# Graph hops with gathering and scattering alternating on the tensor engine: one change and its blind prediction

## The chip, the cores and the metric

The kernel runs on one core of a Trainium2 chip. A core has five engines with a queue of instructions each: PE (the tensor engine: matmuls, with separate loads of their stationary matrix, "PEld" in the profile), DVE (the vector engine), ACT (the scalar engine), POOL (GpSimd) and SP (the sync engine, used here to issue DMAs). They wait for one another through semaphores. PE reads SBUF and writes PSUM; DVE and ACT read PSUM and write SBUF. The metric is the time of one execution in microseconds (us) on the device. An instruction's time in the profile is from its start to its end; on one engine the next may start before the last has ended.

## What is computed

The reference takes 10,000 nodes with 128 features and 160,000 directed edges. It makes seven "hops", each a sum over incoming edges, and then runs a small attention over the eight vectors (input and seven hops) of each node.

```python
h = x
toks = [x]
for _ in range(K):                                   # K = 7
    msg = h[src] * deg_inv_sqrt[src, None] * deg_inv_sqrt[dst, None]
    h = _segment_sum(msg, dst, N)
    toks.append(h)
tok = jnp.stack(toks, axis=1)                        # (N, 8, 128)
t = _layernorm(tok)
q, key, v = t @ wq, t @ wk, t @ wv
o = tok + (softmax(q @ key.T / sqrt(D)) @ v) @ wo    # per node, over its 8 tokens
alpha = softmax(_layernorm(o) @ w_r)
out = sum over the 8 tokens of alpha * o
```

The edges are the same in each hop. The change touches hops 2 to 7 only (and the copies of hop 1).

## The kernel before

**Tables and tiles.** The node values of a hop lie in SBUF as a table `tab` of 79 tiles of 128 nodes. Each value is kept as two float16 numbers, a high half and a low half, so an entry has 256 columns. Two tables take turns: a hop reads one and writes the other.

**A hop as matmuls.** For each of the 79 tiles of destination nodes, the edges into it were sorted once into 18 "slot tiles" of 128 edges; slot tile J takes 32 edges from each of four table tiles. What does not fit goes through two indirect DMAs (the "fetched" rows, `og`). One matrix `w` per destination tile, in 8-bit floats and with only zeros and ones, holds everything: 19 scatter matrices of 128x128 and 72 gather matrices of 128x32. It is stored in DRAM in hop 1 (`gsd`) and read back by SP in each later hop, into one of five buffers.

- *Gather* (L578): four matmuls with 128x32 matrices pick the 4 x 32 rows of one slot tile out of four table tiles and put them side by side into a PSUM tile `p`. Two slot tiles make a pair, with one `p` (128 x 512); nine pairs make a destination tile. There are six `p` buffers.
- *Copy* (L581): ACT or DVE copies `p` to an SBUF buffer `eb`, as float16. There are fourteen of these.
- *Scatter* (L554): one matmul with a 128x128 matrix adds a slot tile of `eb` into the PSUM tile `acc` (two buffers) of the destination tile. The two fetched tiles are added in the same way (L540; L567 for the first two tiles of a hop, whose second fetch comes late, as `ogl`).

**Closing a tile.** DVE adds the two halves of `acc` to `s` (L569). ACT makes the high half of the next table's entry (L610), DVE the low half (L611) and the largest magnitude per row (L612). The finished rows are stored to DRAM (`tabd`, L159, and for the first seven tiles also `tabh`, L163) for the indirect DMAs of the next hop; ACT issues that store. POOL scales `s` to the hop's result `r` (L619), and SP stores it (`tok`, L621).

**What sets the order.** In `block`, hops 2 to 7 call for all nine gathers of a tile in one run (`runs` is `(9,)`). Then `begin` opens `acc` with the fetched rows, and what is pending is scattered, except for the last two pairs, which with the closing step stay pending until after the next tile's gathers. At the end of a hop everything pending is worked off. ACT has pairs 0, 2, 4, 5 and 7 of a tile, DVE 1, 3, 6 and 8. A scheduler places the instructions on their queues; each queue then runs in its order. For a tile in the middle of a hop the queues hold:

- PE: 72 gather matmuls, 2 fetched, 18 scatter (the first four of them belong to the tile before).
- DVE: three copies, one copy, `s`, low half, maximum.
- ACT: five copies, high half, row store.
- POOL: a one-column copy that times the next fetch (L523), one indirect DMA, another one, `r`.
- SP: load of `w`, store of `tok`.

At a hop's start the scale of the next table is made from the maxima of the last one (`scale`), with small steps on DVE and PE, and the first tiles wait for the last rows of the hop before to land in `tabd`.

## Time and profile before

Three runs took 4150.82, 4152.88 and 4153.82 us, median 4152.88. The profiled execution is another one; its span, from the first to the last instruction of the program, is 4139.7 us, at a mean granted tensor clock of 0.976.

| engine | busy us | share of the span | instructions |
|---|---|---|---|
| PE matmul | 3818.7 | 92% | 69690 |
| PE load | 3021.9 | 73% | 69690 |
| DVE | 3355.8 | 81% | 6960 |
| ACT | 2692.1 | 65% | 6830 |
| POOL | 1769.2 | 43% | 2342 |

The preparation and hop 1 last until about 1200 us, hops 2 to 7 until about 3460 us, and the rest is mostly the attention. A row of the groups gives line, engine, operation, tiles (out<-in), shapes and count, then after a bar the busy time in us and the mean of one in ns, then after another bar the idle time of the engine just before and what ended it. A row of a timeline gives start and duration in us, engine, line, operation and count, and in brackets the idle time before it. "128*32" at a matmul is the shape of its stationary matrix. A shape such as 128x256 behind it is that of the result's free size. "Issue" as a releaser means that the engine waited for nothing the profile can name.

### The profile page before, as it was taken

What the parts mean: (1) busy time and instruction counts of PE and PEld (TensorE: products, weight loads), DVE (VectorE), ACT (ScalarE), POOL (GpSimd) and SP (SyncE); (2) the same over time, 40 slices, a digit from 0 to 9 for tenths busy, and PEclk for the clock granted to TensorE, in tenths of its full rate; (3) what the DMA queues carried; (4) which work ended last, traced back from release to release, by engine and by line L of the source; (5) the groups of instructions that cost most, each with busy time, mean ns of one, the idle gap of its engine ahead of it and who ended that gap; (6) DMA issues with size and microseconds to landing.
All of it is one profiled execution on the core that took longest, in us unless ns stands there. A gap on an engine that the chain in (4) does not pass through costs nothing. (4 is left out here: it accounts for less than half of the span.)

```text
span 4139.7 us, 164058 instructions
## 1 busy us (share of the span) xinstructions
PE 3818.7 (92%) x69690; PEld 3021.9 (73%) x69690; DVE 3355.8 (81%) x6960; ACT 2692.1 (65%) x6830; POOL 1769.2 (43%) x2342
## 2 busy tenths in 40 slices
PE   5886889999989999999999999999999999999997
PEld 4665666666657777777777777777777887788785
DVE  8998999999967777777677777777775665999998
ACT  6883456666656665666566566656665657888885
POOL 0000333343345555555555555555555663222222
PEclk8998999999999999999999999999999999999998
DMA  3000444554556665665566656656666653222220
GB/s 109 23 2 17 143 148 153 152 157 150 158 163 185 186 184 180 185 185 184 179 184 186 181 183 186 186 176 186 187 185 191 188 184 105 75 72 81 72 77 17
DMA packets 321181, 594.87 MB, mean 144 GB/s; under 512 B 56183, under 2 KB 214101, under 8 KB 315189
## 3 DMA queue, kind: packets, MB, share of 16 engines
q1 hardware_dynamic: 220565, 478.42, 37.0%
q0 software_dynamic: 35392, 72.55, 6.4%
q10 hardware_dynamic: 64480, 33.33, 2.8%
q8 instruction: 546, 8.95, 0.9%
q14 instruction: 198, 1.62, 0.1%
HBM read 455.43 MB, written 128.67 MB: 141 GB/s over the span
## 5 line engine op out<-in xcount | busy, mean ns | idle before, releaser
L581 ACT CAST eb<-p 128x512 f16<-128x512 f32 x3065 | 1591.8, 600 | 670.9 <-PE p L578 575.6
L581 DVE CAST eb<-p 128x512 f16<-128x512 f32 x1912 | 1263.9, 688 | 439.1 <-PE acc L554 271.6
L578 PE MATMUL p<-tab,w 128*32 128x256 f16 x39816 | 1371.3, 275 | 105.0 <-ACT eb L581 38.1
L578 PEld LDWEIGHTS <-w 128*32 128x32 fp8e4 x39816 | 999.0, 96 | 406.7 <-issue 349.4
L554 PE MATMUL acc<-eb,w 128*128 128x256 f16 (+1 forms) x9954 | 1247.3, 274 | 9.2 <-ACT eb L581 2.3
L554 PEld LDWEIGHTS <-w 128*128 128x128 fp8e4 x9954 | 953.8, 98 | 172.7 <-issue 57.4
L524 POOL DMA_INDIRECT og<-tabh,oidx x553 | 616.6, 1115 | 769.2 <-DVE vi L476 389.0
L524 POOL DMA_INDIRECT og<-tabd,oidx x541 | 584.0, 1080 | 599.9 <-PE acc L554 262.7
L610 ACT ACTIVATE tab<-s,c 128x128 f16<-128x128 f32 x395 | 158.7, 402 | 359.7 <-DVE eb L581 262.9
L619 POOL TENSOR_SCALAR r<-s,ctok 128x128 f32<-128x128 f32 x474 | 295.7, 624 | 45.3 <-DVE s L569 28.2
L611 DVE SCALAR_TENSOR_TENSOR tab<-s,c,tab 128x128 f16<-128x128 f32 x395 | 139.0, 352 | 182.8 <-issue 166.5
L523 POOL COPY og<-eb 128x1 f16<-128x1 f16 x452 | 84.0, 186 | 422.7 <-ACT eb L581 422.7
L569 DVE TENSOR_REDUCE s<-acc 128x128 f32<-128x256 f32 x553 | 228.9, 414 | 23.1 <-PE acc L567 10.1
L991 ACT ACTIVATE junk<-tab 128x128 f32<-128x128 f32 x625 | 245.2, 394 | 0.0
L338 ACT ACTIVATE rs<-iof,rb 128x128 fp8e4<-128x128 f32 x784 | 231.9, 393 | 0.3
L512 DVE TENSOR_TENSOR w<-dsl,iof 128x2432 fp8e4<-128x2432 f16 x79 | 211.6, 2678 | 0.0
L977 PEld LDWEIGHTS po<-v,pT 128*128 128x128 f32 x1250 | 159.3, 193 | 43.6 <-issue 27.8
L966 PE MATMUL pv<-Wv,xT 128*128 128x131 f32 x1250 | 175.9, 283 | 2.5 <-ACT xT L946 1.5
L1049 POOL TENSOR_TENSOR p<-e,in 128x512 f32<-128x512 f32 (+1 forms) x40 | 40.8, 1021 | 320.7 <-DVE e L1047 320.7
L977 PE MATMUL po<-v,pT 128*128 128x128 f32 x1250 | 166.9, 277 | 7.0 <-DVE tab L983 5.4
L966 PEld LDWEIGHTS pv<-Wv,xT 128*128 128x128 f32 x1250 | 152.9, 191 | 19.3 <-issue 8.3
L540 PE MATMUL acc<-og,w 128*128 128x256 f16 x553 | 156.6, 283 | 0.0
(284 smaller groups left out, 4598.7 us busy)
## 6 DMA issues: line engine op xcount, KB each, us to landing
w<-gsd SPq DMA_DIRECT2D x474, 592.0 KB
gsd<-w SPq DMA_DIRECT2D x79, 592.0 KB
rb<-srow SPq DMA_DIRECT2D x79, 576.0 KB
tok<-r SPq DMA_DIRECT2D x546, 64.0 KB
tab<-tok SPq DMA_DIRECT2D x273, 128.0 KB
tabd<-tab ACTq DMA_DIRECT2D x395, 64.0 KB
og<-tabh,oidx POOLq DMA_INDIRECT x553
og<-tabd,oidx POOLq DMA_INDIRECT x541
```

The source lines that it names most:

```text
L338: A.activation(ro[:, j - a, i, :], self.iof, AF.Abs_reciprocal_sqrt, scale=2.0 ** 21, bias=rb[:, j - VP, i:i + 1], saturate=False)
L512: V.tensor_tensor(w[:, :NJ * 128].rearrange("p (j d) -> p j d", d=128), dsl[:, g, :, None].to_broadcast([128, NJ, 128]), self.iof1[:, None ...
L524: self.nc.gpsimd.indirect_dma_start(out=o, out_offset=None, in_=src[0] if i == NI else src[1], in_offset=bass.IndirectOffsetOnAxis(ap=self ...
L554: T.matmul(acc[0][:, :m], w[:, J * 128:(J + 1) * 128], e[:, j, :m], start=first and J == 0, stop=J == NG - 1 and not (first or late))
L569: V.tensor_reduce(s, acc[0][:, 0:256].rearrange("p (h d) -> p d h", h=2), axis=X, op=ALU.add)
L578: T.matmul(p[32 * q:32 * q + 32, j], w[:, NJ * 128 + s * CAP:NJ * 128 + (s + 1) * CAP], tab[:, s, :], start=True, stop=True)
L581: (A.copy if evac(jj) else V.tensor_copy)(e[:, :n, 0:256], p[:, :n].rearrange("p j h d -> p j (h d)"))
L610: self.nc.scalar.activation(new[:, t, 0:128], s, AF.Copy, scale=c)
L619: self.nc.gpsimd.tensor_scalar(r, s, ct[:, t:t + 1], None, op0=ALU.mult)
L966: T.matmul(p[:, g - a, :], S[i]["xT"][:, g, :], Wv, start=True, stop=True)
L977: T.matmul(p[:, g - a, :], PT[i % 2][:, g, :], S[i]["v"][:, g, :128], start=True, stop=True)
L991: A.activation(j, S[i]["x"][:, g, :], AF.Square, bias=S[i]["x"][:, g, 0:1], scale=-1.0, accum_out=S[i]["sq"][:, g:g + 1])
```

## The change

Hop 1 keeps `block`. Hops 2 to 7 get a function of their own, `flow`. It does this:

- It alternates pair by pair: gather a pair, then scatter the pair four places earlier (`LAG`), across the borders of tiles and of hops. Nothing is worked off at a hop's end but the last.
- Each 128x128 scatter matrix, and each of the two fetched ones, is cut into four 128x32 matrices (`quarters`), each with a quarter of the result's partitions, at the same four places in the array that the gather uses. All matmuls of hops 2 to 7 (but a few small ones at a hop's start) thus have one shape.
- ACT copies the even pairs (0, 2, 4, 6, 8), DVE the odd ones. DVE's copy is written as a product with a column of ones, in `block` too.
- A tile's close is followed by `r` at once; the high half of the entry comes one pair later, the low half, the maximum and the store of the rows two pairs later (`steps`). SP issues that store instead of ACT.

```diff
-            (A.copy if evac(jj) else V.tensor_copy)(e[:, :n, 0:256], p[:, :n].rearrange("p j h d -> p j (h d)"))
+            pv = p[:, :n].rearrange("p j h d -> p j (h d)")
+            if evac(jj):
+                A.copy(e[:, :n, 0:256], pv)
+            else:
+                V.tensor_tensor(e[:, :n, 0:256], pv, self.one[:, :, None].to_broadcast([128, n, 256]), op=ALU.mult)
...
+    def flow(self, n, t, w, tab, og, pend, steps, evac, fin, late, mid, ahead, after):
...
+        def quarters(out, W, rows, start, stop):
+            for q in range(0, 128, 32):
+                T.matmul(out[q:q + 32], W[:, q:q + 32], rows, start=start, stop=stop, tile_position=(0, q))
+
+        def fetched(i, start=False, stop=False):
+            W = w[:, (NG + i) * 128:(NG + i + 1) * 128] if i < NI else self.Sov[:, t, :]
+            quarters(acc[0], W, og[i], start, stop)
+
+        def scat(e, jj):
+            if not acc:
+                acc.append(self.pacc.tile([128, 512], F32, name="acc", tag="acc")[:, :256])
+                for i in range(NI if late else NI + 1):
+                    fetched(i, start=i == 0)
+            for j in range(e.shape[1]):
+                J = 2 * jj + j
+                quarters(acc[0], w[:, J * 128:(J + 1) * 128], e[:, j, :256], False, J == NG - 1 and not late)
...
+        for jj in range(-(-NG // 2)):
...
+            for step in steps:
+                step[0] -= 1
+            while steps and not steps[0][0]:
+                steps.pop(0)[1]()
+            pend.append((1, lambda e=e[:, :m], jj=jj: scat(e, jj)))
+            while pend and (not pend[0][0] or sum(k for k, _ in pend) > LAG):
+                pend.pop(0)[1]()
...
-                def fin(t, s, acc, k=k, ct=ct, last=last, i=i):
+                def fin(t, s, k=k, ct=ct, last=last, i=i):
+                    self.token_out(k, t, s, ct)
                     if not last:
-                        self.entries(t, s, i)
-                        self.rows(1 - i, self.tab[1 - i], t, t + 1, nc.scalar)
-                    self.token_out(k, t, s, ct)
+                        steps.append([1, lambda: self.entries_hi(t, s, i)])
+                        steps.append([2, lambda: (self.entries_lo(t, s, i), self.rows(1 - i, self.tab[1 - i], t, t + 1, nc.sync))])
...
-                    for _ in self.block(t, w, tab, og[n], pend, 2, (9,), False, lambda jj: jj in (0, 2, 4, 5, 7), fin, n == 0, n < 2,
-                                        (lambda part, n=n: scale(part, n)) if n < 2 and not last else None,
-                                        lambda after=None, n=n: ahead(n, after), after):
-                        pass
-                while pend:
-                    pend.pop(0)()
+                    self.flow(n, t, w, tab, og[n], pend, steps, lambda jj: jj % 2 == 0, fin, n < 2,
+                              (lambda part, n=n: scale(part, n)) if n < 2 and not last else None,
+                              lambda after=None, n=n: ahead(n, after), after)
+            while pend:
+                pend.pop(0)[1]()
```

In the order built from this, DVE's queue holds per tile: copy 3, `s`, low half, copy 5, maximum, copy 7, and the next tile's copies 1 and 3. SP's holds the load of a `w`, the store of `tok`, the store of the rows.

More of the change, by code (lines that the diff above doesn't have):

```diff
@@ L36 @@
 KO = 8
+LAG = 4
 BIG = 32768.0
@@ L75, in __init__ @@
         V.memset(self.ones32, 1.0)
+        self.one = cp.tile([128, 1], F32, name="one")
+        V.memset(self.one, 1.0)
         self.ones16 = cp.tile([128, 1], F16, name="ones16")
@@ L605, in block, with close @@
             yield
-    def entries(self, t, s, i):
+    def flow(self, n, t, w, tab, og, pend, steps, evac, fin, late, mid, ahead, after):
+        V, A, T = self.nc.vector, self.nc.scalar, self.nc.tensor
+        acc = []
+        def quarters(out, W, rows, start, stop):
[12 more added lines that the diff above has]
+                quarters(acc[0], w[:, J * 128:(J + 1) * 128], e[:, j, :256], False, J == NG - 1 and not late)
+        def close():
+            if late:
+                fetched(NI, stop=True)
+            s = self.fp.tile([128, 128], F32, name="s")
+            V.tensor_reduce(s, acc[0].rearrange("p (h d) -> p d h", h=2), axis=X, op=ALU.add)
+            fin(t, s)
+        for jj in range(-(-NG // 2)):
+            m = min(2, NG - 2 * jj)
+            p = self.pg.tile([128, 2, 2, 128], F32, name="p")
+            for j in range(m):
+                for q in range(4):
+                    s = 4 * (2 * jj + j) + q
+                    T.matmul(p[32 * q:32 * q + 32, j], w[:, NJ * 128 + s * CAP:NJ * 128 + (s + 1) * CAP], tab[:, s, :], start=True, stop=True)
+            e = self.ebuf[self.eb_i % len(self.ebuf)]
+            self.eb_i += 1
+            pv = p[:, :m].rearrange("p j h d -> p j (h d)")
+            if evac(jj):
+                A.copy(e[:, :m, 0:256], pv)
+            else:
+                V.tensor_tensor(e[:, :m, 0:256], pv, self.one[:, :, None].to_broadcast([128, m, 256]), op=ALU.mult)
+            if jj == 0 and not late:
+                ahead(e[:, 0, 0:1])
+            for step in steps:
[5 more added lines that the diff above has]
+                pend.pop(0)[1]()
+            if jj == 4 and n == 1 and mid:
+                mid(0)
+        if n == 0 and mid:
+            mid(0)
+            mid(1)
+        if late:
+            ahead()
+        if after:
+            after[1]()
+        pend.append((0, close))
@@ L609, in entries, with entries_hi, entries_lo @@
+    def entries_hi(self, t, s, i):
+        self.nc.scalar.activation(self.tab[1 - i][:, t, 0:128], s, AF.Copy, scale=self.c1[i][:, t:t + 1])
+    def entries_lo(self, t, s, i):
         c, new = self.c1[i][:, t:t + 1], self.tab[1 - i]
-        self.nc.scalar.activation(new[:, t, 0:128], s, AF.Copy, scale=c)
         self.nc.vector.scalar_tensor_tensor(new[:, t, 128:256], s, c, new[:, t, 0:128], op0=ALU.mult, op1=ALU.subtract)
@@ L699, in run @@
             self.more_ebufs(c.enter_context(tc.tile_pool(name="eb2", bufs=1)), 9, False)
-            pend = []
+            pend, steps = [], []
             for k in range(2, nhop + 1):
```

## The prediction

> **What bounds the kernel now.** I read the stretches first, cut at the first finished sum (`s`) of each hop, then the timeline of one tile, then hop 7's tile against it, then the groups. The first and the last hop's stretch and the sum of all six (busy us and count of PE, PEld, DVE, ACT, POOL; clock, DMA share, GB/s):

> ```profile
> 1206.70:1587.40 380.70, 366.60 (x7314) 294.59 (x7306) 281.08 (x573) 232.87 (x474) 218.49 (x312) 1.00 0.60 184
> ...
> 3112.30:3458.80 346.50, 341.98 (x7089) 287.28 (x7081) 223.99 (x387) 202.87 (x385) 212.41 (x307) 0.99 0.59 182
> sum 2252.10, PE 2168.31 PEld 1753.48 DVE 1620.89 ACT 1367.05 POOL 1302.51; mean PE 361.38 PEld 292.25 DVE 270.15 ACT 227.84 POOL 217.09
> ```

> Hops 2 to 7 take 2252.1 us, 79 tiles each. PE is nearly always busy, at full clock; the others are not. But PE's busy time holds the latencies of matmuls that overlap, so one tile's timeline has to say what PE lacks:

> ```profile
> 2501.31 0.41 DVE L569 TENSOR_REDUCE s<-acc 128x128 f32<-128x256 f32 x1
> 2501.76 0.40 ACT L610 ACTIVATE tab<-s,c 128x128 f16<-128x128 f32 x1 [0.99 <-DVE eb L581]
> 2501.96 1.31 PEld L578 LDWEIGHTS <-w 128*32 128x32 fp8e4 x49 [0.21 <-issue]
> 2501.96 2.53 PE L578 MATMUL p<-tab,w 128*32 128x256 f16 x72
> ...
> 2502.19 0.35 DVE L611 SCALAR_TENSOR_TENSOR tab<-s,c,tab 128x128 f16<-128x128 f32 x1 [0.47 <-issue]
> 2502.46 0.28 DVE L612 TENSOR_REDUCE mx<-tab 128x1 f32<-128x128 f16 x1
> 2502.57 0.35 ACTq L159 DMA_DIRECT2D tabd<-tab  x1
> 2502.63 0.32 SPq L621 DMA_DIRECT2D tok<-r  x1
> 2502.70 2.04 DVE L581 CAST eb<-p 128x512 f16<-128x512 f32 x3
> 2502.96 2.54 ACT L581 CAST eb<-p 128x512 f16<-128x512 f32 x5 [0.81 <-PE p L578]
> 2503.60 0.60 PEld L578 LDWEIGHTS <-w 128*32 128x32 fp8e4 x23 [0.33 <-issue]
> ...
> 2504.42 0.10 PEld L540 LDWEIGHTS <-w 128*128 128x128 fp8e4 x1 [0.21 <-issue]
> ...
> 2504.65 2.13 PE L554 MATMUL acc<-eb,w 128*128 128x256 f16 x18
> 2505.43 0.69 DVE L581 CAST eb<-p 128x512 f16<-128x512 f32 x1 [0.69 <-PE acc L554]
> ...
> 2506.04 0.41 DVE L569 TENSOR_REDUCE s<-acc 128x128 f32<-128x256 f32 x1
> ```

> A tile lasts 2506.04 - 2501.31 = 4.73 us. The loads idle 0.21 us at each change between 128x32 and 128x128 matrices, and the gather's loads break off after 49, until 2503.60. The cause of the break is on ACT: it runs the entry (2501.76), its row store then has to wait for DVE's low half (2502.19) and is issued at 2502.57, and only behind it comes the first copy, at 2502.96, 1.0 us after the gather began. By then six `p` buffers are full and the seventh pair waits. Hop 7, which makes no entries, shows the tile without that:

> ```profile
> 3300.08 2.15 PE L578 MATMUL p<-tab,w 128*32 128x256 f16 x72
> ...
> 3302.39 2.13 PE L554 MATMUL acc<-eb,w 128*128 128x256 f16 x18
> 3304.45 2.15 PE L578 MATMUL p<-tab,w 128*32 128x256 f16 x72
> ```

> Here a tile takes 4.37 us. Eighteen full matrices cost (2.13 - 0.27)/17 = 0.109 us each, where 0.27 is one matmul's latency; eighteen groups of four quarter matrices (2.15 - 0.28)/17 = 0.110, less a trifle for the staggered starts, so 0.109 again. A tile is 18 gathered, 18 scattered and 2 fetched: PE's pure work is 38 x 0.1093 = 4.15 us. The rest of hop 7's tile, 0.22, is the two changes of shape; 4.73 - 4.37 = 0.36 is the wait behind the row store.

> **The change, part by part.**

> *Quarters in place of full matrices.* The 20 matrices of 128x128 become four 128x32 each: PE's matmuls with their loads go from 2 x 92 = 184 to 2 x 160 = 320 a tile. New is that all four of a group stream the same rows, which no gather does. The attention does, in L1003:

> ```profile
> L997 PE MATMUL ps<-xT,uT 128*32 128x32 f32 x5000 | 51.3, 198 | 0.3
> ...
> L1017 DVE TENSOR_TENSOR c<-ps,in 128x512 f32<-128x512 f32 x39 | 26.5, 679 | 0.0
> L1003 PE MATMUL sm<-rb,same 128*32 128x256 f32 x312 | 25.1, 391 | 2.6 <-DVE rb L1010 2.6
> ```

> Its 312 are 78 groups of four, two to a visit: (25.1 - 39 x 0.39)/39 = 0.25 us for the second group, in f32. Were the four to take turns, one would have to pass in 0.06 us, and no 256 columns in these rows do. Bounds of a scatter group: 0.109, below which no 256 columns in these rows go, and 0.25. I take 0.109, the gather's, which has our types and lengths. [...]

> *One shape within a tile.* Two changes go, 0.22 us in each of 474 tiles. If turning from gathering to scattering cost something by itself, less would go; I take the whole.

> *Alternation, four pairs apart.* PE's order becomes gather j, scatter j-4. From a gather's last issue to its scatter there are now 8 x 0.219 = 1.75 us. The copy between needs 0.16 (rest of the matmul's 0.27) + 0.69 and two hand-overs of 0.05 (ACT's first copy ends at 2502.96 + 0.60, the loads go on at 2503.60): 0.95. So DVE or ACT may be 0.8 us late before PE feels it.

> *The entry split, its row store on SP.* ACT loses the 0.35 us issue and the wait ahead of it, so the 0.36 goes unless something else is late. SP gets the store between a token store and a load of `w`, 0.32 + 0.35 + 0.32 us of issues in 4.15. Behind its wait for the low half stands that load:

> ```profile
> w<-gsd SPq DMA_DIRECT2D x474, 592.0 KB
> ```

> It has five buffers and so some 3.6 tiles, 15 us, to land; 592 KB at the 184 GB/s of the stretch are 3.3 us, which is what a tile would pay at worst if that cover were gone. DMA must move the same bytes in 4.15 for 4.73: 210 GB/s, share 0.68, not full. In the first seven tiles a second store goes the same way.

> What is late next is DVE. Its order per tile is: copy 3, `s`, low half, copy 5, maximum, copy 7, copies 1 and 3. Start to start by the rows: copy 0.61 (2505.43 to 2506.04), `s` to low half 0.88 (with ACT's entry between), low half 0.27, maximum 0.24. Sum 4 x 0.61 + 0.88 + 0.27 + 0.24 = 3.83, under 4.15. The tightest place is copy 7. Counted from the last issue of gather 3 it is ready at 0.21 + 0.61 + 0.88 + 0.27 + 0.61 + 0.24 + 0.69 + 0.05 = 3.56 us; its scatter is due at 4 x 0.437 + 0.22 + 1.75 = 3.72. It fits, with 0.16 to spare. ACT and POOL do too: ACT has five copies of 0.604 and the entry's 0.40, 3.42; POOL's stretch gives 218.49/79 = 2.77.

> *Copies as products.* L1017 is such a product (f32 from PSUM by a broadcast), 679 ns, against 688 for the copy:

> ```profile
> L581 DVE CAST eb<-p 128x512 f16<-128x512 f32 x832 | 553.2, 688 | 163.6 <-PE acc L554 130.2 <-PE p L578 18.4 <-remote 4.6
> L581 ACT CAST eb<-p 128x512 f16<-128x512 f32 x1039 | 530.1, 604 | 195.1 <-PE p L578 181.2 <-DVE eb L581 9.0 <-remote 3.3
> ```

> Nine ns on an engine with time left: nothing. In hop 1 only the last quad's copies are DVE's.

> *Hop edges.* A hop costs 380.7 - 79 x 4.73 = 7 us over its tiles, hop 7 346.5 - 79 x 4.37 = 1.3. The emptying of the pipeline at each end goes. The first tiles of a hop must still wait until the last rows have landed and been gathered:

> ```profile
> 1963.59 2.13 PE L554 MATMUL acc<-eb,w 128*128 128x256 f16 x18
> 1968.44 0.27 PE L567 MATMUL acc<-ogl,Sov 128*128 128x256 f16 x1 [2.73 <-DMA ogl<-tabd,oidx]
> ```

> The store now shares SP's queue with the loads of `w` and may land later. Between 0 and 10 us a hop; I take 6, near what it is.

> *Sum.* 474 x 4.153 + 6 x 6 = 2005 us against 2252: 247 saved. The span 4139.7 becomes 3893. The median of the runs, 4152.9, stands 13.2 above the profiled span (what lies around it), so about **3905 us**.

> **The rivals.**

> *DVE becomes the bound.* For: by whole durations its tile is 4 x 0.69 + 0.41 + 0.35 + 0.28 = 3.80 and the 0.47 of waiting for ACT's entry, 4.27 us, and copy 7 has 0.16 to spare. Against: the rows overlap. Time: 395 tiles x (4.27 - 4.15) = 47 more, 3952. If a stall of the entry's size merely moves and 4.37 stands in all tiles, 474 x 0.22 = 104 more, 4009.

> *PE's instructions come too slowly (the slower side).* 320 in 4.15 us is one in 13.0 ns; today's mean is 4.73/184 = 26, the break-even 4.73/320 = 14.8.

> ```profile
> PE 3818.7 (92%) x69690; PEld 3021.9 (73%) x69690; DVE 3355.8 (81%) x6960; ACT 2692.1 (65%) x6830; POOL 1769.2 (43%) x2342
> ...
> q8 instruction: 546, 8.95, 0.9%
> ```

> These 139,380 in 546 packets make 255 a packet; 0.9% of 16 x 4139.7 us is 1.1 us each. One in 3.3 us will be needed. For: if a packet is asked for only when the last is used up, and takes as long as the late gather took from issue to use (1963.70 + 0.94 to 1968.44, 3.8 us), a tile takes 320/255 x 3.8 = 4.77 us: 395 x 0.04 + 79 x 0.40 = 47 over today, 4200.

> ```profile
> 1963.70 0.94 POOL L524 DMA_INDIRECT ogl<-tabd,oidx  x1 [3.18 <-DMA tabd<-tab]
> ```

> It decides from 3.77 us a packet on. Against: a transfer of 1.1, and L997, whose 10,000 matmuls and loads pass in 51 us, 5 ns each, though in short runs. [...]

> *The turns stay dear.* If each of 18 turns between gathering and scattering cost the 0.1 of a change of shape, a tile would take 4.15 + 1.8 = 5.95: 395 x 1.22 + 79 x 1.58 = 607 more, 4760. No row shows such a price without a change of shape.

> *Nothing changes:* the 0.36 and the 0.22 would both have to come back as another wait; 4153.

> **How the numbers follow.** My forecast 0.65 (3870 to 3935: edges of 0 to 10 us, tiles of 4.15 to 4.20); DVE or a moved stall 0.21 (3935 to 4015); instructions 0.09; dear turns 0.03; nothing 0.02. The range, 3870 to 4015, takes in the first two. A measurement here tells a change from none at about 0.2%, 8 us. Faster 0.86, same 0.02, slower 0.12.

> **What will show it.** Right: PE without L578's pauses, groups of both kinds 0.109 apart, `s` every 4.15 to 4.20 us in all six hops, their stretches near 2005 in sum, hardly any "issue" ahead of the loads, no store behind ACT's entry. Wrong: scatter groups wider than 0.109; PE waiting for DVE's `eb`; PE idle on "issue" in every tile; edges over 10 us.

## The result

The changed kernel takes 4436.44 us (median of 4 runs, 4434.8 to 4443.86), the kernel before 4153.23 on the same chip: a ratio of 1.0688, 95% interval 1.0673 to 1.0703. It is 283 us slower where 248 us faster was forecast, and outside the range.

All of it lies in hops 2 to 7. These are their stretches after, from the first `s` of a hop to that of the next, in the columns used before (hop 2, hop 7, the sum):

```profile
1201.80:1627.10 425.30, 374.69 (x12028) 323.29 (x12020) 278.24 (x573) 241.04 (x475) 217.35 (x311) 1.00 0.53 166
...
3339.40:3752.90 413.50, 363.59 (x11740) 314.73 (x11730) 239.06 (x386) 211.53 (x385) 210.85 (x305) 1.00 0.49 152
sum 2551.10, PE 2237.59 PEld 1932.61 DVE 1621.65 ACT 1416.69 POOL 1301.66; mean PE 372.93 PEld 322.10 DVE 270.28 ACT 236.11 POOL 216.94
```

2551.1 us against 2252.1, 299 more; the rest of the span became 5 us shorter. The clock is full (1.00), DMA carries less than before (0.53 for 0.60 in hop 2), DVE and ACT have more idle time than before (busy for 1621.65 and 1416.69 us of 2551.1, before for 1620.89 and 1367.05 of 2252.1). The median time from one `s` to the next is 5.29 us in hops 2 to 6 and 5.27 in hop 7, against 4.73 and 4.37: hop 7, which makes no entries, is no longer shorter, so neither the closing nor ACT's store sets the tile. The page's groups and its instruction queue say who waits for whom:

```profile
PE 3882.9 (88%) x98130; PEld 3199.2 (72%) x98130; DVE 3358.4 (76%) x6961; ACT 2742.7 (62%) x6830; POOL 1772.3 (40%) x2340
...
q8 instruction: 768, 12.58, 1.2%
...
L649 PE MATMUL p<-tab,w 128*32 128x256 f16 x34128 | 1997.8, 274 | 185.2 <-issue 179.4
L621 PE MATMUL acc<-eb,w 128*32 128x256 f16 x34128 | 2015.1, 274 | 115.1 <-issue 100.4
L654 ACT CAST eb<-p 128x512 f16<-128x512 f32 x2370 | 1299.7, 590 | 1147.1 <-PE p L649 948.1
L656 DVE TENSOR_TENSOR eb<-p,one 128x512 f16<-128x512 f32 x1896 | 1302.9, 687 | 456.1 <-PE p L649 395.9
L621 PEld LDWEIGHTS <-w 128*32 128x32 fp8e4 x36024 | 1329.4, 97 | 287.0 <-issue 249.4
L649 PEld LDWEIGHTS <-w 128*32 128x32 fp8e4 x34128 | 1201.0, 97 | 322.1 <-issue 318.2
```

The first line shows a count that the prediction has wrong. PE's matmuls went from 69690 to 98130, 60 more in each of the 474 tiles: 152 for 92 (72 gathered, 72 scattered, 8 fetched). With their loads that is 304 instructions a tile; the prediction, and the expectations after it, say 320.

ACT and DVE wait for PE (`p`, 948.1 and 395.9 us), and PE waits for nothing that has a name: 568 us of "issue" ahead of its loads of `w`. So one of the prediction's own signs of error is there, "PE idle on 'issue' in every tile", and the first reading was its second rival: PE's instructions come too slowly. One tile's timeline says something narrower. PE, its loads, and the other engines around the two stalls of a tile:

```profile
2502.20 0.59 ACT L654 CAST eb<-p 128x512 f16<-128x512 f32 x1 [0.29 <-PE p L649]
...
2502.44 1.02 POOL L527 DMA_INDIRECT og<-tabh,oidx  x1 [0.27 <-POOL og L526]
2502.51 0.47 PE L649 MATMUL p<-tab,w 128*32 128x256 f16 x8
...
2503.06 0.24 PEld L649 LDWEIGHTS <-w 128*32 128x32 fp8e4 x7
...
2503.75 0.09 PEld L649 LDWEIGHTS <-w 128*32 128x32 fp8e4 x1 [0.45 <-issue]
...
2503.76 0.42 DVE L640 TENSOR_REDUCE s<-acc 128x128 f32<-128x256 f32 x1 [0.49 <-PE acc L621]
...
2503.91 0.59 ACT L654 CAST eb<-p 128x512 f16<-128x512 f32 x1 [1.12 <-PE acc L621]
...
2504.19 0.94 POOL L527 DMA_INDIRECT og<-tabd,oidx  x1 [0.73 <-PE p L649]
...
2504.39 0.40 ACT L679 ACTIVATE tab<-s,c 128x128 f16<-128x128 f32 x1
...
2504.56 0.36 PEld L621 LDWEIGHTS <-w 128*32 128x32 fp8e4 x7
...
2504.83 0.35 DVE L684 SCALAR_TENSOR_TENSOR tab<-s,c,tab 128x128 f16<-128x128 f32 x1 [0.64 <-ACT tab L679]
...
2505.55 0.09 PEld L621 LDWEIGHTS <-w 128*32 128x32 fp8e4 x1 [0.63 <-issue]
```

Three things are to be seen. Between the stalls PE is as quick as forecast: eight matmuls of either kind start every 0.22 us. Each stall begins in the middle of a group, where no instruction waits for anything, and ends 1.31 (2503.75 - 2502.44) and 1.36 us (2505.55 - 2504.19) after the start of one of POOL's two indirect DMAs. And PE's signals come late too: the gather that starts at 2502.51 ends at 2502.98, but ACT, free since 2502.20 + 0.59, copies its result only at 2503.91; the `s` at 2503.76 had its last matmul before that gather. ACT's signal to DVE, 0.60 us after the second start, passes in 0.04 us (2504.39 + 0.40 to 2504.83). From 1700 to 3700 us, 90% of 731 indirect DMAs find PE's loads standing still 1.28 us after their start, and 3% at 1.45.

### The profile page after: what moved, and what is told of

Read it like the earlier page. It is cut to its first block, busy times and chain, and to the rows that moved or that the text cites. A ratio compares the mean times of both kernels' runs of the same rounds, so it can differ in the third digit from the quotient of the medians.

```text
span 4434.0 us, 222332 instructions
## 1 busy us (share of the span) xinstructions
PE 3882.9 (88%) x98130; PEld 3199.2 (72%) x98130; DVE 3358.4 (76%) x6961; ACT 2742.7 (62%) x6830; POOL 1772.3 (40%) x2340
## 4 chain that ended last, share of the span: by engine, by line
PE 68%; DVE 17%; issue 8%; ACT 3%; DMA 2%; SPq 0%; ACTq 0%; POOL 0%; DVEq 0%; POOLq 0%
PE acc L621 26%; PE p L649 24%; PE pv L1038 3%; DVE w L515 3%; PE po L1049 3%; PE pu L1027 3%; DVE ux L220 2%; ACT rs L341 2%; DVE o L213 2%; PE pt L1017 2%; DVE oh L207 1%; DVE R L213 1%; PE tb L441 1%; DVE w L512 1%; PE acc L557 1%
## 5 line engine op out<-in xcount | busy, mean ns | idle before, releaser
L649 PE MATMUL p<-tab,w 128*32 128x256 f16 x34128 | 1997.8, 274 | 185.2 <-issue 179.4
L621 PE MATMUL acc<-eb,w 128*32 128x256 f16 x34128 | 2015.1, 274 | 115.1 <-issue 100.4
L654 ACT CAST eb<-p 128x512 f16<-128x512 f32 x2370 | 1299.7, 590 | 1147.1 <-PE p L649 948.1
L656 DVE TENSOR_TENSOR eb<-p,one 128x512 f16<-128x512 f32 x1896 | 1302.9, 687 | 456.1 <-PE p L649 395.9
L621 PEld LDWEIGHTS <-w 128*32 128x32 fp8e4 x36024 | 1329.4, 97 | 287.0 <-issue 249.4
L649 PEld LDWEIGHTS <-w 128*32 128x32 fp8e4 x34128 | 1201.0, 97 | 322.1 <-issue 318.2
L586 ACT CAST eb<-p 128x512 f16<-128x512 f32 x695 | 376.6, 590 | 127.0 <-PE p L581 112.4
L581 PE MATMUL p<-tab,w 128*32 128x256 f16 x5688 | 249.6, 277 | 19.6 <-ACT eb L586 13.5
L557 PE MATMUL acc<-eb,w 128*128 128x257 f16 x1422 | 231.7, 278 | 8.9 <-DVE indeg L716 3.1
L640 DVE TENSOR_REDUCE s<-acc 128x128 f32<-128x256 f32 x474 | 197.6, 417 | 23.6 <-PE acc L621 21.2
L581 PEld LDWEIGHTS <-w 128*32 128x32 fp8e4 x5688 | 130.7, 95 | 95.8 <-issue 78.5
L621 PE MATMUL acc<-og,w 128*32 128x256 f16 x1896 | 170.9, 274 | 4.1 <-issue 3.8
## 6 DMA issues: line engine op xcount, KB each, us to landing
w<-gsd SPq DMA_DIRECT2D x474, 592.0 KB
gsd<-w SPq DMA_DIRECT2D x79, 592.0 KB
```

The costliest lines, as they stand in the source:

```text
L581: T.matmul(p[32 * q:32 * q + 32, j], w[:, NJ * 128 + s * CAP:NJ * 128 + (s + 1) * CAP], tab[:, s, :], start=True, stop=True)
L586: A.copy(e[:, :n, 0:256], pv)
L621: T.matmul(out[q:q + 32], W[:, q:q + 32], rows, start=start, stop=stop, tile_position=(0, q))
L649: T.matmul(p[32 * q:32 * q + 32, j], w[:, NJ * 128 + s * CAP:NJ * 128 + (s + 1) * CAP], tab[:, s, :], start=True, stop=True)
L654: A.copy(e[:, :m, 0:256], pv)
L656: V.tensor_tensor(e[:, :m, 0:256], pv, self.one[:, :, None].to_broadcast([128, m, 256]), op=ALU.mult)
```

## The experiments

They ran on several chips of one type, and these fall into two kinds, which the kernel before tells apart by itself: 4130 to 4154 us on the chip of the record and on three of the five chips of the experiments (the first kind), 3945 and 3951 us on the other two (the second kind). Each chip was used at one time only, so whether a kind belongs to the chip or to the hour no run shows. A time without an interval is of a single run; where a kernel ran four times or more on one chip, its runs lie within 16 us. A run is compared with the kernel before on its own chip. "Hops" is the time from the first `s` of hop 2 to the last of hop 7, "tile" the median from one `s` to the next; the mean, hops / 474, is larger, since stalls fall unevenly on the tiles.

| run | us | kernel before there | hops | tile |
|---|---|---|---|---|
| the record: changed kernel | 4436.4 | 4153.2 | 2551.1 | 5.29 |
| e7_no_w_loads | 4378.4 | 4138.8 | 2497.6 | 5.21 |
| h2_direct | 4206.1 | 4150.3 | 2327.7 | 4.65 |
| h1_neither | 3919.9 | 4150.3 | 2045.3 | 4.15 to 4.38 |
| h3_before_nofetch | 3949.7 | 4150.3 | 2076.5 | 4.37 |
| h5_before_sp | 3991.1 | 4135.1 | 2110.7 | 4.37 |
| h4_before_quarters | 4427.9 | 4135.1 | 2542.5 | 5.16 |
| second kind: before_again | 3950.9 | 3950.9 | 2089.5 | 4.37 |
| after_again | 4197.6 | 3950.9 | 2337.1 | 4.67 |
| e1_nofetch | 4155.8 | 3945.3 | 2298.3 | 4.65 |
| e4_onefetch | 4217.9 | 3945.3 | 2353.8 | 4.67 |
| e2_direct | 4213.7 | 3945.3 | 2351.0 | 4.67 |
| e3_before_quarters | 4212.7 | 3945.3 | 2352.3 | 4.57 to 4.79 |
| e5_before_sp | 3948.8 | 3950.9 | 2088.3 | 4.37 |
| e6_after_full | 4761.7 | 3950.9 | 2900.6 | 6.12 |

Theory A: PE's instructions come too slowly. Theory B: each of POOL's indirect DMAs holds PE up. Theory C: the alternation itself is dear.

**The indirect DMAs taken away, wholly, by half, or made plain; the quarters alone.**

```diff
 def fetch(...):
+    return self.ogc                                    # e1_nofetch: a tile of zeros
+    if i < NI: return self.ogc                         # e4_onefetch: the tabd one stays
+    self.nc.sync.dma_start(o, src_rows[r:r + 128, :])  # e2_direct: 128 rows that lie in a row
```

```diff
-                T.matmul(acc[0][:, :m], w[:, J * 128:(J + 1) * 128], e[:, j, :m], ...)
+                quarters(acc[0][:, :m], w[:, J * 128:(J + 1) * 128], e[:, j, :m], ...)   # e3, in the kernel before
```

> The changed kernel without the two indirect DMAs of a tile in hops 2 to 7: the fetched matmuls stay, but stream one constant tile of zeros, so the edges that are fetched are left out of the sums. PE's instructions are as many as before it (320 a tile). Theory A, PE's instructions come too slowly (5.29 us / 320 = 16.5 ns each): nothing changes, tiles of 5.3 us, about 4436 us. Theory B, each indirect DMA on POOL holds PE up for about 0.57 us (half of 5.29 - 4.15): tiles of 4.15 to 4.25 us and 4436 - 474 x 1.1 = about 3915 us. Theory C, the alternation itself is dear (signals between PE, ACT and DVE): nothing changes.

> As the run without indirect DMAs, but the second of the two (from tabd) stays, the first (from tabh) is left out together with its edges. Theory A and C: 5.3 us a tile, about 4436 us. Theory B: one hold-up of 0.57 us is left in a tile, 4.15 + 0.57 = 4.72 us, 4436 - 474 x 0.57 = about 4166 us.

> The changed kernel with both indirect DMAs replaced by plain DMAs that SP issues: the same 128 rows of 512 bytes into the same buffers, but rows that lie in a row instead of the indexed ones, so the fetched edges get wrong values. [...] Theory A and C: 5.3 us a tile, about 4436 us. Theory B, if it is POOL's making of descriptors that holds PE up: 4.15 to 4.3 us a tile, 3915 to 3990 us. Theory B, if it is the arrival of the rows: near 5.3 us, 4436 us.

> The kernel before with one part of the change alone: the scattered and fetched matrices of hops 2 to 7 in four quarters each, in the old order, nothing alternating. 320 PE instructions a tile, but the 18 scattered matrices in a row signal nothing between them. Theory A: 320 x 16.5 ns = 5.3 us a tile, 4153 + 395 x 0.56 + 79 x 0.92 = about 4445 us. Theory B, if PE is held because its instructions stop coming while POOL makes descriptors: two holds of about 0.5 us a tile, some 5.0 to 5.2 us, 4270 to 4390 us. Theory B, if PE is held only because its signals do not get out: few holds, the change of shape (0.22) is saved, 4.5 us a tile, 4153 - 474 x 0.22 = about 4050 us. Theory C: as that, about 4050 us.

They fell on a chip of the second kind, and there theory B was wrong: with no indirect DMA, with one, or with plain ones, a tile takes 4.65 to 4.67 us, and the quarters in the old order take as long. What is common to the four is 304 PE instructions a tile. Their stalls do not keep to a place in the tile; in the first of them (PE's loads, without indirect DMAs) they look so:

```profile
2103.38 0.12 PEld L651 LDWEIGHTS <-w 128*32 128x32 fp8e4 x8 [0.35 <-issue]
2103.50 0.21 PEld L623 LDWEIGHTS <-w 128*32 128x32 fp8e4 x8
...
2106.56 0.22 PEld L651 LDWEIGHTS <-w 128*32 128x32 fp8e4 x8
2107.67 0.12 PEld L623 LDWEIGHTS <-w 128*32 128x32 fp8e4 x8 [0.90 <-issue]
```

From the end of one stall to the beginning of the next there are 128 loads and as many matmuls, 256 instructions, and so it goes on: some 420 stretches between 1300 and 3400 us are of just 256, and most of the others of a multiple. The records of the instruction queue's transfers (in the record 768 for 2 x 98130 instructions, 255.6 to one), laid beside it, give the way of one packet (means over packets that end in a stall): from PE's entering 256 instructions to the start of the transfer of the next 256, 1.64 us; the transfer, 1.15; from its end to their first instruction, 1.39. Together 4.17 us, while PE works off 256 instructions in 3.49 (32 groups of 0.109). The packet that PE will need sets out only after PE has entered the one before, and comes 0.7 us too late. Hops 2 to 7 hold 561 packets: 2298.3 us are 4.10 each.

**Both kernels on such a chip; whole matrices; the row store alone.** The e5 edit:

```diff
-                        self.rows(1 - i, self.tab[1 - i], t, t + 1, nc.scalar)
+                        self.rows(1 - i, self.tab[1 - i], t, t + 1, nc.sync)
```

and e6 makes `quarters` one matmul with the whole matrix, in the changed kernel.

> The kernel before, unchanged, for its trace on the chip of these runs: in the first experiments it took 3945.3 us there, 208 less than in the runs of the record. If that chip's tiles lack the hold behind the indirect DMAs, hops 2 to 7 have tiles of about 4.73 - 208/474 = 4.3 us; if the chip is quicker in all stages, the preparation and the attention are shorter in the same ratio (5%).

> The changed kernel, unchanged, on the same chip as the rest of these runs. Theory A2 (PE's instructions arrive in packets of 256, and a packet takes about 3.74 us or more whatever PE does): stalls 256 instructions apart, tiles of 4.67 us as without the indirect DMAs, about 4215 us. Theory B (a hold at each indirect DMA): stalls at the same two places of each tile, 5.3 us a tile, about 4436 us.

> The changed kernel with one part undone: the scattered and fetched matrices are whole 128x128 matrices again, the alternation pair by pair stays. 184 PE instructions a tile in place of 320, but 18 changes of shape. Theory A2: 184 / 256 x 3.74 = 2.7 us a tile of supply, no longer the limit; what is left is 4.15 us and 18 changes of 0.1 us each, 5.95 us a tile, if a change of shape is what costs 0.1 (about 4750 us); if those 0.2 us a tile were the emptying of the pipeline and not the shape, 4.2 us a tile and some 3900 to 4000 us. Theory C (the alternation is dear): 5.3 us or more.

> The kernel before with one part of the change alone: SP issues the store of the finished rows in hops 2 to 7 in place of ACT. Where ACT's first copy waits behind that store, 0.36 us a tile are saved in hops 2 to 6: 395 x 0.36 = 142 us less than the kernel before on the same chip. If the stall only moves (to DVE or to a signal of PE that comes late), no change.

The changed kernel is slower on this kind too, 4197.6 against 3950.9, with stalls 256 instructions apart and none tied to the indirect DMAs; its packets need 1.76 + 1.08 + 1.38 = 4.2 us, and 2337.1 us over 561 packets are 4.17 each. In e6, 184 instructions a tile, no stall of that kind is left, but a tile takes 6.12 us: 4.15 and 18 turns of 0.109. PE's loads and matmuls there:

```profile
2500.10 0.12 PEld L648 LDWEIGHTS <-w 128*32 128x32 fp8e4 x8 [0.21 <-issue]
...
2500.43 0.11 PEld L620 LDWEIGHTS <-w 128*128 128x128 fp8e4 x2 [0.21 <-issue]
...
2500.76 0.12 PEld L648 LDWEIGHTS <-w 128*32 128x32 fp8e4 x8 [0.21 <-issue]
```

A turn costs that only where the shape changes; the same turns in quarters cost nothing between stalls (in e1 groups of both kinds, in turn, start every 0.22 us). So theory C falls, and the quarters do what they are for.

The row store alone changed nothing here (3948.8 us for 3950.9). The kernel before on this chip, on DVE, PE and POOL, shows why:

```profile
2501.20 2.15 PE L578 MATMUL p<-tab,w 128*32 128x256 f16 x72
...
2501.94 2.48 DVE L581 CAST eb<-p 128x512 f16<-128x512 f32 x4 [0.51 <-PE p L578]
...
2502.77 1.02 POOL L524 DMA_INDIRECT og<-tabh,oidx  x1 [0.27 <-POOL og L523]
```

DVE's four copies, that of pair 8 the last, pass without a break, and the closing is early enough that ACT's store does not delay its first copy. A tile takes 4.37 us in all six hops. On the chip of the record, that copy began only at 2505.43, 0.69 us idle for PE (a row the prediction shows), and POOL had started this:

```profile
2504.07 1.02 POOL L524 DMA_INDIRECT og<-tabh,oidx  x1 [0.27 <-POOL og L523]
```

That is again 1.36 us after the start of an indirect DMA, and 88% of 363 such DMAs between 1300 and 3050 us have DVE's next copy 1.25 to 1.5 us after their start (none of 431 on the other chip). So the hold was in the kernel before, on that chip; there it kept back one signal, not PE.

**The loads of `w` taken away; turns of two tiles.**

```diff
+                    if len(keep) < 5:                  # e7, in the changed kernel: five matrices, used in turn
+                        keep.append(self.gsp.tile(..., name=f"w{len(keep)}")); nc.sync.dma_start(keep[-1], self.GSd[t])
+                    w = keep[n % 5]
```

```diff
-            while len(pend) > lag:                     # e9, in the kernel before with e5's edit;
+            while len(pend) > lag and not hold:        # hold on every other tile; 22 eb, 5 og buffers
```

> The changed kernel without the loads of w in hops 2 to 7: five matrices are loaded at the start of hop 2 and used in turn, so the sums are of the wrong edges; 592 KB of DMA traffic a tile go, PE's instructions stay as many and as they are. Theory A2a (the packets of 256 instructions are late because their transfers wait behind the loads of w: 1.76 us from a packet's beginning on PE to the start of the next transfer, where the least is 1.1): the start falls to 1.1 to 1.2 us, the way around to about 3.55 us, hardly any stalls, 4.2 to 4.4 us a tile, some 4198 - 474 x 0.5 = about 3960 us. Theory A2b (a packet's way is that long whatever the traffic): stalls of 0.7 us as before, 4.67 us a tile, about 4200 us.

> Not a part of the change but the other way to fewer changes of shape: the kernel before with whole matrices, in turns of two tiles (gather both, then scatter both; 22 eb buffers, five og buffers, rows stored by SP). 184 PE instructions a tile as before, half the changes of shape. If a change costs 0.109 us, as 18 of them gave 6.12 - 4.15 = 1.97 us a tile with whole matrices alternating, and the supply of 184 instructions is no limit: 4.37 - 0.109 = 4.26 us a tile, 474 x 0.109 = 52 us less than the kernel before on the same chip, ratio 0.987. If the fetched rows or w come late in turns of two: 4.4 us or more, no gain.

These came to a chip of the first kind, so the first could not tell what it was made for. It told something else: with almost no DMA traffic left (share 0.20) the stalls sit at the same two places of each tile as in the record, and 93% of the indirect DMAs find PE standing still 1.28 us after their start; 5.21 us a tile. With the queue this quiet the fetched rows can be told apart too: their packets start from 1.6 us after the start of their DMA, when PE already runs again. So it is not the arrival of the rows that holds PE. The turns of two tiles took 4207.3 us, ratio 1.0165 (1.0148 to 1.0182), and 4206.4 in h6 on another chip of that kind, 1.0175 (1.0158 to 1.0192): both `tabh` fetches now fall into the gathers. In one pair of tiles DVE's next copy starts 1.38 us after one of them, and PE's loads then stand still for 0.57 us until that copy is done. The edit holds that of e5 as well; against e5's edit alone on the chip of h6 (3991.1 us, below) the turns cost 215 us. On the second kind of chip they were not run.

**The first kind of chip: neither cause, one cause, and the kernel before.**

> The changed kernel without the loads of w (five matrices in turn) and without the indirect DMAs (fetched matmuls stream zeros): the wrong edges are summed and the fetched ones are left out, PE's instructions stay 320 a tile. On a chip where the kernel before takes some 3950 us (packets of 256 instructions come late there, no hold behind the indirect DMAs): if late transfers are the loads' doing, 4.2 to 4.4 us a tile, about 3950; if a packet's way is what it is, 4.6 us, some 4150. On a chip where the kernel before takes some 4140 us: if PE is held behind POOL's indirect DMAs (theory B), the two stalls a tile (1.1 us) go, tiles of 4.2 to 4.6 us against 5.21 without the loads alone, 4378 - 474 x (0.6 to 1.0) = 3900 to 4090 us; if not, 5.2 us and 4378.

> The changed kernel with both indirect DMAs of a tile as plain DMAs by SP of rows that lie in a row (wrong rows, same traffic), as run before on another chip, where tiles took 4.67 us with them and without. On a chip where the kernel before takes some 4140 us: if POOL's making of the descriptors holds PE, the stalls at two places of each tile go and those 256 instructions apart are left, 4.67 us a tile, 4436 - 474 x 0.62 = about 4140 us; if the arrival of scattered rows does, 5.2 us, about 4400 us. On a chip where it takes some 3950: 4214 us again.

> The kernel before without the indirect DMAs of hops 2 to 7 (fetched matmuls stream zeros, the fetched edges are left out). On a chip where the kernel before takes some 4140 us: theory B says that the copy of pair 8 and the closing no longer come late behind the indirect DMAs, so that a tile falls from 4.73 to the 4.37 of the other chips, 4140 - 395 x 0.36 = about 4000 us, and less by the waits at a hop's start. If PE is not held by them, 4.73 us a tile and no change but at a hop's start (some 20 us). On a chip where it takes some 3950: 4.37 us a tile and at most 30 us less, at the hops' edges.

The edits are those of e1 and e7 together, of e2, and of e1 in the kernel before. Theory B holds here. Plain DMAs of the same size bring the tile from 5.29 to 4.65 us, with stalls 256 instructions apart as on the other chips. PE's loads run on through both plain DMAs, 128 of them from one stall to the next:

```profile
2107.93 0.23 PEld L653 LDWEIGHTS <-w 128*32 128x32 fp8e4 x8
...
2108.71 0.42 SPq L529 DMA_DIRECT2D og<-tabd  x1
...
2109.89 0.32 SPq L529 DMA_DIRECT2D og<-tabh  x1
...
2111.13 0.30 PEld L653 LDWEIGHTS <-w 128*32 128x32 fp8e4 x8
...
2112.77 0.20 PEld L625 LDWEIGHTS <-w 128*32 128x32 fp8e4 x8 [1.34 <-issue]
```

So it is the indirect DMA on POOL that holds PE, not the amount of traffic. What POOL does in the 0.94 to 1.02 us of such a DMA no trace shows; that it makes descriptors is a guess of the expectations. The kernel before without these DMAs takes 4.37 us a tile, as on the second kind of chip, and 3949.7 us in all. Without the loads of `w` as well, the changed kernel comes near its forecast: 3919.9 us for 3905, hops of 2045.3 for 2005. That is only 30 us below the kernel before without its indirect DMAs (h3): of the 248 us that were forecast, the 142 for the row store lay in a wait that the hold makes. Two successive fetched groups on PE's loads:

```profile
2103.98 0.19 PEld L623 LDWEIGHTS <-w 128*32 128x32 fp8e4 x4
...
2108.13 0.19 PEld L623 LDWEIGHTS <-w 128*32 128x32 fp8e4 x4
```

4.15 us, 304 instructions, 13.7 ns each. In the packets that still end in a stall (some 200) the transfer starts 1.20 us after PE enters the packet before, against 1.81 in h2 on the same chip; transfer and the rest are the same (1.14 and 1.39 against 1.07 and 1.40). What makes packets late is the start of their transfer among other DMA traffic (share 0.13 in h1, 0.59 in h2). h1 leaves out the loads and the fetched rows together; the loads alone were not taken away where no hold is.

**What the hold stops; the row store where the hold is.**

> The kernel before with its scattered and fetched matrices of hops 2 to 7 in quarters, nothing alternating, as run before on a chip without the hold (4.67 us a tile there, stalls 256 instructions apart). On a chip where the kernel before takes some 4140 us: if POOL's indirect DMA stops PE's instructions, its loads stand still up to 1.35 us behind the start of each, as in the changed kernel, and a tile takes 5.2 us or more, about 4430 us; if it only keeps PE's signals back, the 72 matmuls of a scatter, which signal next to nothing, run on, and the stalls stay 256 instructions apart: 4.7 to 4.9 us a tile, 4150 to 4250 us.

> The kernel before with the store of the finished rows on SP in place of ACT, in hops 2 to 7, the same kernel that changed nothing on a chip without the hold (3948.8 against 3950.9 us). On a chip where the kernel before takes some 4140 us the closing comes late behind the hold, and ACT's first copy behind the store: with the store gone from ACT the 0.36 us a tile of the prediction should go, 395 x 0.36 = 142 us, to about 4000, ratio 0.966. If the late copy of pair 8 shows elsewhere (DVE, then PE), less of it goes: at the worst no change. On a chip where it takes some 3950: no change.

> The turns of two tiles again, which lost 1.65% on a chip with the hold. On a chip where the kernel before takes some 3950 us: half the changes of shape, 474 x 0.109 = 52 us less, ratio 0.987; if the fetched rows or w come late in turns of two, no gain. On a chip where it takes some 4140 us: the ratio of 1.0165 again.

The quarters in the old order signal next to nothing in a scatter, and stand still all the same (h4, PE's loads and POOL):

```profile
2503.39 1.02 POOL L524 DMA_INDIRECT og<-tabh,oidx  x1 [0.27 <-POOL og L523]
...
2503.90 0.34 PEld L539 LDWEIGHTS <-w 128*32 128x32 fp8e4 x10
...
2504.69 1.21 PEld L539 LDWEIGHTS <-w 128*32 128x32 fp8e4 x46 [0.46 <-issue]
...
2505.17 0.94 POOL L524 DMA_INDIRECT og<-tabd,oidx  x1 [0.77 <-PE acc L539]
...
2506.48 0.37 PEld L539 LDWEIGHTS <-w 128*32 128x32 fp8e4 x16 [0.58 <-issue]
```

The stalls end 1.30 and 1.31 us after the two starts. So the hold stops PE's instructions, not only its signals. The kernel before runs through it: a matrix and its load every 0.109 us are some 18 instructions in that microsecond, quarters with 0.22 us for eight 73. That fits a hold of the supply, with the loads in hand running on for 0.7 to 0.9 us, but no run tests it.

The row store on SP alone: 3991.1 us, ratio 0.9653 (0.9632 to 0.9673), 144 us less than the kernel before; 142 were expected. Its rows on ACT, DVE, PE and POOL, from one closing to the next:

```profile
2422.01 0.41 DVE L569 TENSOR_REDUCE s<-acc 128x128 f32<-128x256 f32 x1
...
2422.46 0.40 ACT L610 ACTIVATE tab<-s,c 128x128 f16<-128x128 f32 x1 [0.51 <-DVE eb L581]
...
2422.70 2.15 PE L578 MATMUL p<-tab,w 128*32 128x256 f16 x72
...
2423.21 2.05 ACT L581 CAST eb<-p 128x512 f16<-128x512 f32 x4 [0.35 <-PE p L578]
...
2424.32 1.02 POOL L524 DMA_INDIRECT og<-tabh,oidx  x1 [0.27 <-POOL og L523]
...
2425.78 0.69 DVE L581 CAST eb<-p 128x512 f16<-128x512 f32 x1 [0.45 <-PE acc L554]
...
2426.39 0.41 DVE L569 TENSOR_REDUCE s<-acc 128x128 f32<-128x256 f32 x1
```

The copy of pair 8 still comes 1.46 us after the indirect DMA's start, but ACT goes straight from the entry to its first copy, and the 72 gather matmuls pass without a break (2.15): 4.38 us. This one line, without the rest of the change, beats both kernels on the first kind of chip and costs nothing on the second.

## Why the prediction was wrong

- **What bounds the kernel now.** The row store behind which ACT's first copy waits was rightly read, and worth what was said: 0.36 us a tile, 144 us (h5). But the row above it, DVE's copy of pair 8 with 0.69 us idle for PE, was quoted and not asked about. Its matmuls had ended 0.9 us before, and it came 1.36 us after POOL's start. It was the one visible trace of the hold, and the reason why the closing was late enough for the store to matter.
- **Quarters at 0.109.** Right: 0.22 us for eight, in every run.
- **One shape, 0.22 saved.** Right: a turn with a change of shape costs 0.109 (e6), a turn without costs nothing (h1, 4.15 us for 38 groups of 0.109).
- **Alternation with 0.8 us of slack, DVE's 3.83 us, products at nothing.** Right as far as the runs reach: h1's tiles of 4.15 us contain all of them, and the product takes 687 ns for the copy's 688. No run tried the products alone.
- **Hop edges at 6 us.** In the changed kernel hops 2 to 6 take 7 to 10 us more than 79 median tiles each; a small error.
- **The sum.** Its 13.2 us around the span are not a cost of launching: the later executions lie about 2 us over their spans (4150.29 us over 4148.5 on the chip of h1 to h3). That alone would have put the forecast some 11 us lower.
- **The step that failed** is "PE's pure work is 38 x 0.1093 = 4.15 us" as the time of a tile, with nothing for the supply of instructions. It is the time PE needs if its instructions are there. h1 shows 4.15 us; 0.5 us more is the late packets (h2, 4.65), and with the indirect DMAs it is 5.29. Over the six hops that is 2045, 2328 and 2551 us. The two do not add: without the traffic of `w`, the hold alone makes 5.21. The likely reason is that a packet goes on arriving while PE is held; transfers do end within holds, in e7 and, as 55 of 439 between 1700 and 3700 us, in the record (0.9 to 1.28 us after a start), but no run separates this.
- **The rival "PE's instructions come too slowly"** had the right mechanism for the second kind of chip: 256 to a packet, the next one under way too late. Its count was wrong. The 20 matrices in quarters are 80 matmuls beside 72, so 304 instructions a tile: one in 13.7 ns, not 13.0, a packet every 3.5 us, not 3.3, and a break-even with the kernel before at 15.6 ns, or 3.97 us a packet, not 14.8 and 3.77. So its 4200 us beside the 4197.6 measured is luck. With 304, its 3.8 us a packet would have given 304/255 x 3.8 = 4.53 us a tile, below the 4.73 of the kernel before. Measured were 4.2 us a packet, 304/256 x 4.2 = 4.99 us, and a mean tile of 2337.1/474 = 4.93, where the kernel before takes 3950.9 and not 4152.9. It got 0.09 on two arguments. "A transfer of 1.1 us" took the transfer for the whole way; it is a quarter of it. "5 ns each in L997" is a rate in short runs, as the prediction half said. On the chip of the record what decides is the hold, and that was no rival at all.

## What to carry to other kernels

Before a matrix is cut into smaller ones, count instructions against supply: 304 on PE in 4.15 us ask for a packet of 256 every 3.5 us, and here, under the loads of `w`, its way took 4.2. An idle time that ends a fixed while after another engine's instruction, in the middle of a group that waits for nothing, may belong to that instruction, whatever the profile calls it; lay the starts of the two side by side, and take that instruction away, before choosing a theory. And try the parts of a change alone: one line of this one was worth 3.5% where the hold is, and the rest cost that and more.
